# Turned token rows by way of DRAM in five transfers a chunk, ordered behind the residual sums

## The chip, the cores and the metric

The kernel runs on one core of one Trainium2 chip. The time is the device time of one execution in microseconds (us). Before the change it is 790.7 us, the median of 3 runs (790.24 to 791.23). Engines are named as in the profile: PE (matrix multiplication, with PEld for its weight loads), DVE or VectorE, ACT or ScalarE, POOL or GpSimd, and SP, which here only issues DMAs.

## The reference

Four layers are applied to x of 2048 tokens x 576 features: linear attention, MLP, linear attention, MLP, each on the layer norm of x and with a residual sum. Both attention layers have the same weights, and so have both MLPs.

```python
def _A_ref(x, wqkv, wo):            # 32 heads of 18
    q, k, v = split(x @ wqkv)
    phi = lambda t: where(t > 0, t + 1, exp(t)) + 1e-6
    pq, pk = phi(q), phi(k)
    kv = einsum("bhsd,bhse->bhde", pk, v);  z = pk.sum over tokens
    num = einsum("bhqd,bhde->bhqe", pq, kv)
    den = einsum("bhqd,bhd->bhq", pq, z)[..., None] + 1e-6
    return (num / den) @ wo
def _B_ref(x, w1, b1, w2, b2):      # 576 -> 4608 -> 576
    h = gelu(layernorm(x) @ w1 + b1)
    return h @ w2 + b2
x = x + _A_ref(_layernorm(x), A_wqkv, A_wo)
x = x + _B_ref(_layernorm(x), B_w1, B_b1, B_w2, B_b2)
x = x + _A_ref(_layernorm(x), A_wqkv, A_wo)
x = x + _B_ref(_layernorm(x), B_w1, B_b1, B_w2, B_b2)
```

## The kernel before

Layers are called 1 to 4 here; in the code `li` runs from 0 to 3. Layers 1 and 3 are attention (`layer_A`), 2 and 4 the MLP (`LayerB`). Tokens go in 16 tiles of 128, and four tiles make a chunk of 512 columns. All weights stay in SBUF. The residual x lives in a DRAM buffer `x_d` in float32; each tile's sum (L379) is stored there by SP (L385) and loaded again where it is needed (L366 for the residual, L265 for a norm).

Every matmul against tokens needs the normed rows turned, features on partitions: that is `yT`, 128 x 5 x 2048. `LNPipe` makes it. An item is a token tile; each `tick` moves every item one stage on: load (L265, where the row is not at hand), statistics (L272, L273, L278, L281/L283), the reciprocal root on POOL (L288), for POOL norms a small product (L292), the norm into `y_ring` (L303 on POOL, L307 on VectorE, with a copy of the last 64 features by POOL, L311), and the turn. There are two ways to turn:

- by PE: five transposes (L324) into a PSUM bank of their own, `ps_tp`, and a copy by ScalarE (L326). Layer 1 does so for all tiles, and the first chunk of each MLP too (fed at L528 from the output stage of the attention layer before).
- by DMA (`turn_rows`): VectorE transposes blocks of 32 x 32 (L225) into the single buffer `turned`; with the fourth tile of a chunk SP issues 16 SBUF to SBUF copies (L232) in pieces of 256 bytes, which put the blocks on the right partitions. The columns of a chunk then stand in another order, which `spread` and `gather` undo where ScalarE reads the result. Chunks 1 to 3 of each MLP and all four chunks of layer 3 take this way: 10 chunks, 160 copies.

An attention layer first makes k, v and q for all tiles, then the denominators (`den_stage`), the scaling (`scale_stage`) and, tile by tile, the output product and its residual sum (`wo_stage`). While the output stage runs, the sums of tiles 0 to 3 are normed and turned for the following MLP, whose first matmul needs all of chunk 0. Sums are written into `xn`, three buffers.

An MLP layer takes each chunk in turn: nine groups of the first product (`m1_group`, 36 matmuls each, L624) with GELU on ScalarE (L620), then four token tiles of the second product (72 matmuls each, L672) and their residual sums. While chunk c is in its first product, `feed_next` sends the rows of chunk c + 1 into `LNPipe`. Only for c = 0 has it `after=dve_last["sum"]`, an order without a semaphore: the loads and statistics of chunk 1 come after the attention layer's last sum. For later chunks there is no such order.

PSUM has eight banks: two pairs for accumulation (`accA`, `accB`), three single banks `ps_h` and one `ps_tp`.

The order of an engine's instructions is fixed when the kernel is built. PE's order is written out by hand (`pe`). On the other queues, SP's among them, a planner goes through the program with estimated durations and lets instructions that it takes to be ready go ahead of earlier ones that wait; `add_manual_dep(..., NOSYNC)` forbids that for one pair. At run time each queue works strictly in that order.

Of the kernel before, what the change touches and what calls it, by code (L numbers as in the profile page):

```python
# [7 lines left out]
ACT = mybir.ActivationFunctionType  # L8
ALU = mybir.AluOpType
BF16 = mybir.dt.bfloat16  # L10
# [24 lines left out]
def build(tc, A_x, A_wqkv, A_wo, B_w1, B_b1, B_w2, B_b2, out, dbg=None, n_layers=4):  # L35
    nc = tc.nc
    dbg = dbg or {}
    with ExitStack() as ctx:
        const = ctx.enter_context(tc.tile_pool(name="const", bufs=1))
        ps_h = ctx.enter_context(tc.tile_pool(name="ps_h", bufs=3, space=PSUM))  # L40
        ps_tp = ctx.enter_context(tc.tile_pool(name="ps_tp", bufs=1, space=PSUM))
# [21 lines left out]
        eps_row = const.tile([1, H], BF16, name="eps_row")  # L63
        one_row = const.tile([1, P], BF16, name="one_row")
# [9 lines left out]
        def inner_diag(tile_, lead, n):  # L74
# [10 lines left out]
            fill(eps_row, 1e-6),  # L85
# [30 lines left out]
        x_d = dpool.tile([NT, P, D], F32, name="x_d")  # L116

# [99 lines left out]
        state = dict(ycnt=0, vcnt=0, xl=0)  # L217
# [3 lines left out]
        def turn_rows(y, t, kind):  # L221

            c, j = divmod(t, TPC)
            nb = 4 * KD if kind == "B" else D // 32
            nc.vector.transpose(out=turned[:, 0:nb, j, :], in_=y[:, 0:32 * nb])  # L225
            if j < TPC - 1:
                return
            for i in range(4):
                for jj in range(4):
                    nk = KD if 16 + jj < nb else KD - 1  # L230
                    cols = slice(c * CB + i * P, c * CB + (i + 1) * P)
                    nc.sync.dma_start(  # L232
                        out=yT[32 * jj:32 * (jj + 1), 0:nk, cols],
                        in_=turned[32 * i:32 * (i + 1), jj:4 * (nk - 1) + jj + 1:4].rearrange("p k t c -> p k (t c)"))
# [8 lines left out]
        class LNPipe:  # L243
# [11 lines left out]
            def tick(self, transposes=1):  # L255
                for it in list(self.items):
# [58 lines left out]
                    elif st == 4:  # L315
                        y = it["y"]
                        t = it["t"]
                        if it["evac"] == "dma":
                            turn_rows(y, t, it["kind"])
                            self.items.remove(it)  # L320
                            continue
                        tp = ps_tp.tile([P, KD, P], BF16, name="tp", tag="tp")
                        for k in range(KD):
                            pe(nc.tensor.transpose(out=tp[:, k, :], in_=y[:, k * P:(k + 1) * P], identity=ident[:]))  # L324
                        if it["evac"] == "act":
                            nc.scalar.copy(out=yT[:, :, t * P:(t + 1) * P], in_=tp[:])  # L326
                        else:
                            nc.vector.tensor_copy(out=yT[:, :, t * P:(t + 1) * P], in_=tp[:])
                        self.items.remove(it)
                        continue  # L330
# [41 lines left out]
        def residual(li, t, halves):  # L372
            xo = xo_of.pop((li, t))
            last = (li == n_layers - 1)
            if last:
                xn = work.tile([P, 2 * D], BF16, name="xbf", tag="xn", bufs=3)[:, 0:D]
            else:
                xn = work.tile([P, D], F32, name="xn", tag="xn", bufs=3)[:]
            total = nc.vector.tensor_tensor(out=xn.rearrange("p (h n) -> p h n", h=2), in0=halves,  # L379
                                            in1=xo.rearrange("p (h n) -> p h n", h=2), op=ALU.add)  # L380
            dve_last["sum"] = total.ins.name
            if last:
                nc.sync.dma_start(out=out_f[t * P:(t + 1) * P, :], in_=xn)
                return None
            nc.sync.dma_start(out=x_d[t], in_=xn)  # L385
            return xn

        def layer_A(li, next_kind, pre_a1=None):
# [129 lines left out]
            def wo_stage(t):  # L518
# [8 lines left out]
                if xn is not None and next_kind == "B" and t < TPC:  # L527
                    lnp.feed(xn, t, "B", "pool", "act")  # L528
# [46 lines left out]
        class LayerB:  # L575
# [7 lines left out]
            def m1_group(self, c, g):  # L583
# [32 lines left out]
                def evict(n):  # L616
                    f = g * GF + n
                    hT[f] = blk.tile([P, D], BF16, name="hT", tag="blk")
                    to, ps = (hT[f][:, 0:CB], dst[n]) if c == 0 else (spread(hT[f][:, 0:CB]), gather(dst[n]))
                    act_last["gelu"] = nc.scalar.activation(out=to, in_=ps, func=ACT.Gelu_apprx_tanh,  # L620
                                                            bias=b1T[:, f:f + 1], scale=1.0).ins.name
# [24 lines left out]
            def run(self):  # L646
                li, next_kind = self.li, self.next_kind

                def feed_next(c, i):
                    if c + 1 < NCB:  # L650
                        t = (c + 1) * TPC + i
                        lnp.feed(None, t, "B", "dve", "dma", load_from=t, after=(dve_last["sum"] if c == 0 else None))

                for c in range(NCB):
# [12 lines left out]
                    for j in range(TPC):  # L667
                        t = c * TPC + j
                        acc = ps_acc.tile([P, 2, 512], F32, name="m2_ps", tag=next_acc())
                        for f in range(NF):  # L670
                            for half in range(2):
                                pe(nc.tensor.matmul(acc[:, half, 0:HALF], lhsT=hT[f][:, j * P:(j + 1) * P],  # L672
                                                    rhs=w2_sb[:, f, half * HALF:(half + 1) * HALF],
                                                    start=(f == 0), stop=(f == NF - 1)))
# [111 lines left out]
```

## Time and profile before

| | |
|---|---|
| median of 3 runs | 790.7 us |
| the profiled execution | 790.27 us, its span 788.6 us |
| granted PE clock, mean | 0.992 |
| busy: PE / VectorE / ScalarE / POOL | 769.9 / 275.4 / 341.7 / 127.0 us |
| first matmul of the MLP (layers 2, 4) | 112.1 and 491.9 us |
| one MLP chunk | 70.4 us: 35 first product, 35.4 second |
| DMA | 63.2 MB, mean 80 GB/s |

The page of the profile gives busy times by engine and slices of the span in tenths. The waits name who waited for whom, in total, how often and the longest. The timelines give start and duration of merged instructions of one engine, and in brackets the idle time ahead of them and who ended it. For SP a line is the time in which it issued such DMAs one after another; the data land later.

### The profile page before, as it was taken

The page shows a single profiled execution, that of the slowest core. Times are in us where ns is not written, and L with a number is a line of the kernel's source. Part 1 is how long each engine was busy: PE and PEld are TensorE (multiplying, and loading weights), DVE is VectorE, ACT ScalarE, POOL GpSimd, SP SyncE. Part 2 cuts the span into 40 slices and gives each one's busy share as a digit, 9 for nine tenths or more (in the row PEclk, how much of TensorE's full clock was granted, in tenths as well). Part 3 has the DMA queues.
Part 4 walks back from the last instruction along what each step waited for, and adds up shares of the span by engine and source line. Part 5 has one row for each costly group of instructions (what it writes and reads, how often), then busy time and mean ns, then how long its engine had stood idle before and what let it go on. Part 6 is the DMA issues. An engine that isn't in the chain of part 4 may idle for free.

```text
span 788.6 us, 15939 instructions
## 1 busy us (share of the span) xinstructions
PE 769.9 (98%) x6613; PEld 496.5 (63%) x6613; DVE 275.4 (35%) x710; ACT 341.7 (43%) x754; POOL 127.0 (16%) x211
## 2 busy tenths in 40 slices
PE   8999999999999999999999999996999999999998
PEld 5776654675477457547777756455744764675476
DVE  6786864044324413301355597544100000000000
ACT  5888636304610650362077774650056016304600
POOL 4671403013000301200000022311110010001000
PEclk9999999999999999999999999998899999999999
DMA  9990473122412331311120028443410110011000
GB/s 265 280 294 5 130 252 91 22 75 66 94 43 69 83 65 46 91 17 31 61 61 2 1 89 288 152 94 79 86 39 1 31 61 2 5 50 38 1 24 23
DMA packets 70642, 63.23 MB, mean 80 GB/s; under 512 B 37418, under 2 KB 55210, under 8 KB 70570
## 3 DMA queue, kind: packets, MB, share of 16 engines
q1 hardware_dynamic: 70570, 62.21, 28.1%
q8 instruction: 52, 0.85, 0.4%
q14 instruction: 20, 0.16, 0.1%
HBM read 39.38 MB, written 16.52 MB: 71 GB/s over the span
## 4 chain that ended last, share of the span: by engine, by line
PE 83%; DVE 7%; DMA 4%; SPq 3%; POOL 1%; issue 1%; ACT 1%; DVEq 0%; POOLq 0%
PE m_ps L672 34%; PE h_ps L624 17%; PE hp_ps L624 14%; PE q_ps L436 5%; PE k_ps L400 5%; PE v_ps L415 3%; SPq L232 3%; PE v_ps L412 2%; PE wo_ps L523 2%; DVE xn L379 1%; DMA x_d<-xn 1%; DVE turned L225 1%; PE kvacc L430 1%; DMA x_ring<-x_d 1%; DVE y_ring L307 1%
## 5 line engine op out<-in xcount | busy, mean ns | idle before, releaser
L672 PE MATMUL m_ps<-w_sb,hT 128*128 128x288 bf16 x2304 | 286.2, 287 | 8.5 <-DVE xbf L379 8.5
L672 PEld LDWEIGHTS <-hT 128*128 128x128 bf16 x2304 | 225.9, 98 | 69.8 <-issue 12.1
L624 PEld LDWEIGHTS <-w_sb 64*128 64x128 bf16 x2304 | 124.4, 94 | 136.6 <-issue 1.9
L624 PE MATMUL hp_ps<-yT,w_sb 64*128 64x512 bf16 x1152 | 178.0, 376 | 0.0
L629 ACT COPY relay_sb<-relay_sb 128x1 f32<-128x1 f32 x144 | 28.5, 198 | 276.6 <-PE h_ps L624 234.7
L624 PE MATMUL h_ps<-yT,w_sb 64*128 64x512 bf16 x1152 | 147.9, 376 | 0.0
L620 ACT ACTIVATE hT<-h_ps,b1T 128x512 bf16<-128x512 f32 x144 | 91.2, 684 | 44.5 <-PE h_ps L624 44.5
L288 POOL TENSOR_TENSOR ln_rstd<-ln_u,neg_half 128x1 f32<-128x1 f32 x64 | 36.2, 567 | 413.9 <-DVE ln_u L281 216.8
L620 ACT ACTIVATE hT<-hp_ps,b1T 128x512 bf16<-128x512 f32 x144 | 91.2, 693 | 0.0
L379 DVE TENSOR_TENSOR xbf<-m_ps,x_ring 128x576 bf16<-128x576 f32 x16 | 12.0, 754 | 221.2 <-PE m_ps L672 221.2
L369 POOL TENSOR_TENSOR x_ring<-x_ring,b_bc 128x576 f32<-128x576 f32 x32 | 41.1, 1291 | 203.7 <-DMA x_ring<-x_d 203.6
L379 DVE TENSOR_TENSOR xn<-m_ps,x_ring 128x576 f32<-128x576 f32 x16 | 12.1, 758 | 155.9 <-PE m_ps L672 155.9
L624 PE MATMUL h_ps<-yT,w_tail 64*128 64x512 bf16 x144 | 54.1, 376 | 0.0
L624 PE MATMUL hp_ps<-yT,w_tail 64*128 64x512 bf16 x144 | 54.1, 376 | 0.0
L436 PE MATMUL q_ps<-yT,wqkv_sb 128*126 128x512 bf16 (+1 forms) x200 | 50.0, 382 | 0.5 <-ACT phi_a L351 0.5
L225 DVE STREAM_TRANSPOSE turned<-y_ring 128x640 bf16<-128x640 bf16 (+1 forms) x40 | 32.2, 812 | 41.8 <-DMA yT<-turned 35.4
L523 PE MATMUL wo_ps<-kvwo,pq 126*128 126x288 bf16 (+1 forms) x320 | 43.7, 285 | 2.1 <-DVE xn L379 1.6
L400 PE MATMUL k_ps<-wqkv_sb,yT 128*128 128x288 bf16 x320 | 44.3, 286 | 0.0
L350 ACT ACTIVATE phi_e<-k_ps 128x288 bf16<-128x288 f32 x64 | 27.0, 421 | 34.8 <-PE k_ps L400 34.7
L352 DVE TENSOR_SCALAR phi_e<-phi_e 128x288 bf16<-128x288 bf16 (+2 forms) x104 | 30.7, 296 | 25.3 <-ACT phi_e L350 24.9
L523 PEld LDWEIGHTS <-pq 126*128 126x128 bf16 (+1 forms) x320 | 30.5, 97 | 13.7 <-issue 3.9
L400 PEld LDWEIGHTS <-yT 128*128 128x128 bf16 x320 | 30.9, 98 | 11.1
(90 smaller groups left out, 625.7 us busy)
## 6 DMA issues: line engine op xcount, KB each, us to landing
x_ring<-x_d SPq DMA_DIRECT2D x72, 288.0 KB, 3.1
x_d<-xn SPq DMA_DIRECT2D x48, 288.0 KB, 2.2
w_sb<-in_B_w_dram SPq DMA_DIRECT2D x6, 864.0 KB, 9.5
yT<-turned SPq DMA_DIRECT2D x128, 40.0 KB, 2.0
w_sb<-in_B_w_dram SPq DMA_DIRECT2D x9, 512.0 KB, 5.5
x<-in_A_x_dram SPq DMA_DIRECT2D x16, 144.0 KB, 4.1
x_ring<-in_A_x_dram SPq DMA_DIRECT2D x16, 144.0 KB, 3.4
out_dram<-xbf SPq DMA_DIRECT2D x16, 144.0 KB, 1.8
```

The costliest lines, as they stand in the source:

```text
L225: nc.vector.transpose(out=turned[:, 0:nb, j, :], in_=y[:, 0:32 * nb])
L288: nc.gpsimd.tensor_tensor(out=rstd[:], in0=it["u"][:], in1=neg_half[:], op=ALU.pow)
L352: nc.vector.tensor_scalar(out=e[0:rows, 0:n], in0=e[0:rows, 0:n], scalar1=1.0, scalar2=1e-6, op0=ALU.min, op1=ALU.add)
L369: nc.gpsimd.tensor_tensor(out=xo, in0=xo, in1=b2_bc[:], op=ALU.add)
L379: total = nc.vector.tensor_tensor(out=xn.rearrange("p (h n) -> p h n", h=2), in0=halves, in1=xo.rearrange("p (h n) -> p h n", h=2), op=ALU ...
L400: pe(nc.tensor.matmul(kp[:, 0:HALF], lhsT=yT[:, k, tok], rhs=wqkv_sb[:, k, D + half * HALF: D + (half + 1) * HALF], start=(k == 0), stop=( ...
L436: pe(nc.tensor.matmul(qp[0:GR[g], :], lhsT=wqkv_sb[:, k, GO[g]:GO[g] + GR[g]], rhs=yT[:, k, c * CA:(c + 1) * CA], start=(k == 0), stop=(k ...
L523: pe(nc.tensor.matmul(wp[:, half, 0:HALF], lhsT=pq[(g, c)][0:GR[g], j * P:(j + 1) * P], rhs=kvwo[g][0:GR[g], half * HALF:(half + 1) * HALF ...
L620: act_last["gelu"] = nc.scalar.activation(out=to, in_=ps, func=ACT.Gelu_apprx_tanh, bias=b1T[:, f:f + 1], scale=1.0).ins.name
L624: mm = pe(nc.tensor.matmul(dst[n], lhsT=wt, rhs=mv, start=(seen[n] == 0), stop=(seen[n] == 8)))
L629: relay = nc.scalar.copy(out=relay_sb[:, 1:2], in_=relay_sb[:, 0:1])
L672: pe(nc.tensor.matmul(acc[:, half, 0:HALF], lhsT=hT[f][:, j * P:(j + 1) * P], rhs=w2_sb[:, f, half * HALF:(half + 1) * HALF], start=(f == ...
```

## The change

All rows of layers 2 to 4 are turned by DMA; layer 1 keeps PE's transposes. The 16 copies of a chunk become four writes to a DRAM buffer `y_d` (two, in turn), one for each 32 partitions of `turned`, and one read of the whole chunk into `yT`, which waits for the four writes. Every turn stands behind the residual sum that was last written in the program (`dve_last["sum"]`, order only), and `feed_next` has `after=dve_last["sum"]` for every chunk. GELU reads chunk 0 in the turned order as it does the others. `ps_tp` goes; `ps_h` has four banks, and layer 1's transposes take theirs from it. The constants `eps_row` and `one_row` of the denominator's last matmuls get 126 rows instead of one, with zeros in all rows of `eps_row` but the first. The last token tile of layer 4 does its 36 matmuls of the first half of columns and then those of the second, and each half has its own sum and its own store.

```diff
-        ps_h = ctx.enter_context(tc.tile_pool(name="ps_h", bufs=3, space=PSUM))
-        ps_tp = ctx.enter_context(tc.tile_pool(name="ps_tp", bufs=1, space=PSUM))
+        ps_h = ctx.enter_context(tc.tile_pool(name="ps_h", bufs=4, space=PSUM))
...
-        eps_row = const.tile([1, H], BF16, name="eps_row")
-        one_row = const.tile([1, P], BF16, name="one_row")
+        eps_row = const.tile([126, H], BF16, name="eps_row")
+        one_row = const.tile([126, P], BF16, name="one_row")
...
-            fill(eps_row, 1e-6),
+            fill(eps_row, 0.0),
+            lambda: nc.gpsimd.memset(eps_row[0:1, :], 1e-6),
...
+        y_d = [dpool.tile([KD, P, CB], BF16, name=f"y_d{i}") for i in range(2)]
...
-        def turn_rows(y, t, kind):
+        def turn_rows(y, t):
 
             c, j = divmod(t, TPC)
-            nb = 4 * KD if kind == "B" else D // 32
-            nc.vector.transpose(out=turned[:, 0:nb, j, :], in_=y[:, 0:32 * nb])
+            turn = nc.vector.transpose(out=turned[:, :, j, :], in_=y[:])
+            if dve_last["sum"] is not None:
+                tc.add_manual_dep(turn.ins, dve_last["sum"], NOSYNC, reason="rows are turned behind the sums")
             if j < TPC - 1:
                 return
+            home = y_d[state["turns"] % 2]
+            state["turns"] += 1
             for i in range(4):
-                for jj in range(4):
-                    nk = KD if 16 + jj < nb else KD - 1
-                    cols = slice(c * CB + i * P, c * CB + (i + 1) * P)
-                    nc.sync.dma_start(
-                        out=yT[32 * jj:32 * (jj + 1), 0:nk, cols],
-                        in_=turned[32 * i:32 * (i + 1), jj:4 * (nk - 1) + jj + 1:4].rearrange("p k t c -> p k (t c)"))
+                nc.sync.dma_start(
+                    out=home[:, :, i * P:(i + 1) * P].rearrange("k (jj r) n -> r (k jj) n", jj=4),
+                    in_=turned[32 * i:32 * (i + 1), :, :, :].rearrange("r j t c -> r j (t c)"))
+            nc.sync.dma_start(out=yT[:, :, c * CB:(c + 1) * CB], in_=home.rearrange("k p n -> p k n"))
...
-                        tp = ps_tp.tile([P, KD, P], BF16, name="tp", tag="tp")
+                        tp = ps_h.tile([P, 512], F32, name="tp", tag="h")
+                        tp = tp[:, 0:DPAD // 2].bitcast(BF16).rearrange("p (k n) -> p k n", k=KD)
...
-            total = nc.vector.tensor_tensor(out=xn.rearrange("p (h n) -> p h n", h=2), in0=halves,
-                                            in1=xo.rearrange("p (h n) -> p h n", h=2), op=ALU.add)
-            dve_last["sum"] = total.ins.name
+            parts = [slice(h * HALF, (h + 1) * HALF) for h in range(2)] if last and t == NT - 1 else [slice(0, D)]
+            for i, cols in enumerate(parts):
+                ps = halves if len(parts) == 1 else halves[:, i:i + 1, :]
+                nh = ps.shape[1]
+                total = nc.vector.tensor_tensor(out=xn[:, cols].rearrange("p (h n) -> p h n", h=nh), in0=ps,
+                                                in1=xo[:, cols].rearrange("p (h n) -> p h n", h=nh), op=ALU.add)
+                dve_last["sum"] = total.ins.name
+                if last:
+                    nc.sync.dma_start(out=out_f[t * P:(t + 1) * P, cols], in_=xn[:, cols])
...
-                    lnp.feed(xn, t, "B", "pool", "act")
+                    lnp.feed(xn, t, "B", "pool", "dma")
...
-                    to, ps = (hT[f][:, 0:CB], dst[n]) if c == 0 else (spread(hT[f][:, 0:CB]), gather(dst[n]))
-                    act_last["gelu"] = nc.scalar.activation(out=to, in_=ps, func=ACT.Gelu_apprx_tanh,
+                    act_last["gelu"] = nc.scalar.activation(out=spread(hT[f][:, 0:CB]), in_=gather(dst[n]),
+                                                            func=ACT.Gelu_apprx_tanh,
...
-                        lnp.feed(None, t, "B", "dve", "dma", load_from=t, after=(dve_last["sum"] if c == 0 else None))
+                        lnp.feed(None, t, "B", "dve", "dma", load_from=t, after=dve_last["sum"])
...
-                        for f in range(NF):
-                            for half in range(2):
-                                pe(nc.tensor.matmul(acc[:, half, 0:HALF], lhsT=hT[f][:, j * P:(j + 1) * P],
+                        by_half = li == n_layers - 1 and t == NT - 1
+                        steps = [(f, half) for half in range(2) for f in range(NF)] if by_half else \
+                            [(f, half) for f in range(NF) for half in range(2)]
+                        for f, half in steps:
+                            pe(nc.tensor.matmul(acc[:, half, 0:HALF], lhsT=hT[f][:, j * P:(j + 1) * P],
...
```

## The prediction

> **What bounds the kernel now.** I read the page first (spans, busy shares, slices), then the list of waits, the timelines of VectorE, SP and PE around the one weak slice, and short windows at the end of the attention layers.
>
> ```profile
> span 788.6 us, 15939 instructions
> ...
> PE 769.9 (98%) x6613; PEld 496.5 (63%) x6613; DVE 275.4 (35%) x710; ACT 341.7 (43%) x754; POOL 127.0 (16%) x211
> ...
> PE   8999999999999999999999999996999999999998
> ```
>
> PE is busy 98% of the span, so only the 18.7 us in which it is idle, and PE work that is removed, can be won. One slice falls to 6 tenths, near 550 us. The waits name its cause (us in total, times, longest):
>
> ```profile
> DVE turned L225 <- DMA yT<-turned: 35.4, 4, 10.3
> ...
> PE m_ps L672 <- DVE xbf L379: 8.5, 1, 8.5
> ```
>
> 8.5 us of PE's idle time is one wait of a second MLP matmul for a residual sum of the last layer. VectorE's timeline (start, us, line, operation, wait before) says why that sum was late:
>
> ```profile
> 537.14 0.58 DVE L307 TENSOR_SCALAR y_ring<-x_ring,ln_mv,ln_rstd 128x576 bf16<-128x576 f32 x1 [0.67 <-POOL ln_rstd L288]
> 545.42 1.57 DVE L225 STREAM_TRANSPOSE turned<-y_ring 128x640 bf16<-128x640 bf16 x2 [7.70 <-DMA yT<-turned]
> ...
> 552.57 1.38 DVE L379 TENSOR_TENSOR xbf<-m_ps,x_ring 128x576 bf16<-128x576 f32 x2
> ```
>
> The sums of tiles 0 and 1 stand behind turns of chunk 3, which is needed 140 us later. Those turns wait until the single buffer `turned` has been read for chunk 2, and SP issues that chunk's copies one by one:
>
> ```profile
> 532.80 10.98 SPq L232 DMA_DIRECT2D yT<-turned  x16
> 543.88 1.01 SPq L265 DMA_DIRECT2D x_ring<-x_d  x2
> 552.71 11.07 SPq L232 DMA_DIRECT2D yT<-turned  x16
> ```
>
> The MLP itself has nothing to give. The places the change can hurt are the ends of the two attention layers, shown here for layer 3 (the second one; PE's timeline, then windows of layers 1 and 3 with PE, PEld, DVE, ACT and POOL busy, granted clock, DMA share, GB/s):
>
> ```profile
> 479.23 0.53 PE L324 MATMUL tp<-ident,y_ring 128*128 128x128 bf16 x5
> 480.01 1.39 PE L523 MATMUL wo_ps<-kvwo,pq 126*128 126x288 bf16 x10 [0.26 <-DVE xn L379]
> ...
> 485.45 6.53 PE L523 MATMUL wo_ps<-kvwo,pq 126*128 126x288 bf16 x50
> 491.91 1.04 PE L624 MATMUL h_ps<-yT,w_sb 64*128 64x512 bf16 x8
> ```
> ```profile
> 104.00:106.00 2.00, 2.00 (x18) 1.51 (x16) 1.66 (x4) 1.39 (x3) 0.00 (x0) 1.00 0.80 251
> 106.00:108.00 2.00, 1.19 (x10) 0.79 (x9) 0.50 (x1) 0.84 (x2) 0.00 (x0) 1.00 0.95 323
> ...
> 486.00:488.00 2.00, 2.00 (x18) 1.58 (x17) 1.37 (x3) 1.72 (x3) 0.00 (x0) 1.00 1.04 408
> 488.00:490.00 2.00, 2.00 (x18) 1.57 (x17) 0.98 (x2) 0.00 (x0) 0.00 (x0) 1.00 1.04 386
> ```
> ```profile
> 553.00:565.00 12.00, 11.66 (x76) 8.49 (x76) 1.20 (x3) 0.00 (x0) 0.00 (x0) 0.78 0.36 58
> ```
>
> Before the first MLP matmul (491.91; after layer 1 at 112.1) the 16 DMA engines are full with residual stores and loads. The last line is a stretch with almost only one chunk's 16 turn copies: 0.36 of 12 us, so 4.3 us of all engines' time, for 0.65 MB in pieces of 256 bytes.
>
> **The change part by part.**
>
> *Order behind the sums.* Loads and statistics of chunks 2 and 3 must now come after the sums of the chunk before, and turns after the sum last written. Nothing of chunk 3 can stand ahead of tile 0's sum: minus 8.5. What is later: the norm of a chunk now starts in its predecessor's MLP. It takes 15 us (497 to 512 on VectorE) and some 10 for the copies, from 8 us into a stretch of 70.4; 37 us to spare, so nothing. I take -8.5; the other end is 0, if another instruction takes the sum's place.
>
> *Five DMAs instead of sixteen, 10 chunks.* SP's share falls from 11 us a chunk to four writes of about 0.6 (row 0.60 each; but three weight loads of 768 pieces took 3.35, 1.1 each, when the engines were full), a wait until they land, and one read. Landing: 2.0 to 2.2 us in calm, 3.2 for stores and 3.9 for loads in the full stretch 476 to 500. A chunk is ready 2.5 + 2.2 + 0.6 + 3.1 = 8.4 us after its last turn, against 11 + 2.0 = 13. For the MLP's chunks 1 to 3 and for layer 3's rows both are hidden: layer 3's last chunk was turned at 398.7 and its k projection comes at 435. Nothing.
>
> *The first chunk of each MLP, now turned too.* Removed: 4 x 5 PE transposes a layer (four steps of 0.28 us between the start of the transposes and that of the next group) and four ScalarE copies of 0.70. Added: four turns of 0.84 on VectorE, which was busy 24.9 of the 30.3 us of this stage; and two trips over DMA, 4.3 us of engine time for the writes (by the row above) and 0.65 MB at 386 GB/s = 1.7 for the read. In layer 3 the turn of tile 3 stands behind the sum of tile 7, which began at 481.53; with the turn of tile 2 ahead of it too, it ends near 484.1 (481.53 + 0.84 + 0.76 + 0.84, and 0.1 of gaps). Behind the turns on VectorE stand the scale products and the sum of tile 8, for which PE waits 0.26 now. Four writes issued to 486.6; landed with 3.2 at 489.8 to 490; read issued 490.5, landed with 3.9 at 494.5. The wo groups alone would let the MLP begin at 492.5 (0.6 late through VectorE), so the copy decides. Behind the read on SP, which waits for the writes, stand the stores of tiles 8 to 12 and their `xn` buffers (three, so the sum of tile 14 waits for the store of 11): that puts PE's second accumulators near the same 494.5. I take +2.8 for layer 3; ends -1.1 (only the PE work is saved) and +6.6 (below). In layer 1 the residual rows that are loaded are bfloat16 and half as long, so the engines are less full, and 1.1 us of PE waiting is there already: turn of tile 3 to 103.1, writes issued to 105.6, landed 108.5, read landed 112.5 to 113, against 112.1. I take +1.0, ends -1.5 and +5.0.
>
> No row shows a write to DRAM in pieces of 256 bytes; nearest are the same pieces between SBUF rows at 4.3 us a chunk (taken) and, as upper end, twice that: the slowest of the 160 old copies landed in 3.8 us against a median of 2.0. The Trainium skill, "DMA: Bandwidth & Descriptors", section "Specifications", says that below 512 bytes the DMA engine does a read-modify-write, and "Why small descriptors are slow (HBM only)" exempts SBUF to SBUF. By that rule the old copies were cheap and the new ones are not, with about 8.6 us for the writes (an estimate), and the time would be the second rival's. No run here shows it.
>
> *Fourth one-bank buffer.* The waits of q_ps for phi_a (0.5 us) end: -0.4. With the transposes' own bank gone, a token tile of layer 1 uses four banks where it used three and one, so nothing is lost; ends 0 and -1.
>
> *`eps_row` over 126 rows.* The four closing matmuls of a denominator took 0.17 us from start to start (469.73 to 469.90), the twenty before them 0.39; at that pace they take 0.08: 8 x 0.09 = 0.7 at most. I take -0.3; ends 0 and -0.7. One more fill on POOL lies in the first weights' time.
>
> *GELU in turned order for chunk 0:* ScalarE was busy 22.7 us in chunk 0 (112 to 147) and 22.3 in chunk 1 (182 to 217), which reads that way already. Nothing.
>
> *Last tile by halves.* The last sum takes 0.76 us, then 1.8 for its store. Half of it takes about 0.4, and the store is half: -0.5; ends 0 and -0.8.
>
> **Sum.** -8.5 - 0.4 - 0.3 - 0.5 + 2.8 + 1.0 = -5.9. The profiled execution took 790.27 (span 788.6 and 1.7 around it), 0.4 below the median of 790.7. That gives 784.4.
>
> **The rivals.**
>
> *Hidden tails.* The two starts of the MLP cost nothing, because the copies land beside the wo groups. For it: 8 us lie between the last turn and 492. Against: the engines at 1.04. The time is 790.3 - 9.7, less half of the 2.2 us of PE transposes: 779.5.
>
> *The small DRAM writes decide (slower).* Place: the last 10 us of both attention layers. At 8.6 us for the writes they land near 494, the read at 498.5 in layer 3: +6.6; in layer 1 +5.0. Total -9.7 + 11.6 = +1.9: 792.2. For it: the engines are full there already. Against: 2560 pieces took only 4.3 us before. It decides as soon as the two starts together come more than 9.7 us later.
>
> *The stall stays or moves.* Another instruction holds the sum of tile 0. Then 790.3 - 1.2 + 3.8 = 792.9. Against: the dependences name exactly the instructions that stood there.
>
> **How the numbers follow.** Chances: forecast 0.54, hidden tails 0.22, small writes 0.16, stall stays 0.08. A difference under 0.2% (1.6 us) is about what can't be told from none. The forecast's own range is 781.5 to 788; with the hidden case below and most of the slower cases it is 778.5 to 792. Faster: 0.54 + 0.22 = 0.76, slightly lowered for an overlap of the small writes' milder half with no change: faster 0.75, same 0.10 (most of it from the small writes), slower 0.15.
>
> **What would show it.** PE's wait for `xbf` is gone and the sums of the last layer's chunk 0 follow their matmuls by under 1 us; the turns of chunk 2 come after 565. SP shows groups of four writes and one read. In the attention layers the first MLP matmul waits for `yT` 1 to 4 us, with the DMA share at 1.0 before it. If the writes land over 5 us after issue, the second rival is right; if the first MLP matmul follows the last wo group at once, the first. I am wrong if the order of the queues changes elsewhere: a residual load or a store put behind the waiting read would stall every later sum.

## The result and the profile after

The changed kernel takes 799.0 us (median of 4 runs, 797.5 to 799.5) where the kernel before takes 790.9 (4 runs beside it, 790.2 to 791.2). The ratio is 1.010, with a 95% interval of 1.0083 to 1.0118: the change makes the kernel slower by 8.1 us. The forecast was 784.4 us, and 792.0 was the top of its range.

The page of the profile after, with the same rows as before and the row of the granted clock in tenths:

```profile
span 797.7 us, 15688 instructions
...
PE 770.2 (97%) x6573; PEld 495.9 (62%) x6573; DVE 278.3 (35%) x719; ACT 335.7 (42%) x746; POOL 126.6 (16%) x212
...
PE   7999869999999999999999997799999999999998
PEclk9999979999999999999999999699999999999999
```

The weak slice at 550 us is gone. Two others have come, near 110 us and from 480 to 518 us, which are the ends of the two attention layers, and in both the granted clock falls too. PE's busy time is what it was (770.2 against 769.9), though 40 matmuls are gone, because the matmuls under the low clock take longer. Cut at PE's first matmul of each layer (starts in its timeline), the two spans compare like this:

| stretch | before | after | difference |
|---|---|---|---|
| start to the k product of tile 3 (17.4 / 18.4) | 17.4 | 18.4 | +1.0 |
| rest of layer 1, to layer 2's first matmul (112.1 / 121.0) | 94.7 | 102.6 | +7.9 |
| layer 2, to layer 3's first matmul (393.8 / 402.7) | 281.7 | 281.7 | 0 |
| layer 3, to layer 4's first matmul (491.9 / 511.9) | 98.1 | 109.2 | +11.2 |
| layer 4 to the end (788.6 / 797.7) | 296.7 | 285.8 | -10.9 |

So the stall that the change removes was worth 10.9 us, and the ends of the attention layers took 19 back. (The first row is not counted as the change's: these k products wait for the first rows of x to be loaded and normed, and tile 3's begins between 17.1 and 20.0 us in the kernels shown here, whatever their edit.)

The waits on the list of after that matter (us in total, times, longest):

```profile
DVE xn L386 <- DMA x_d<-xn: 18.9, 7, 4.7
PE wo_ps L531 <- DVE xn L386: 16.7, 11, 4.0
```

Before, these two were 4.3 and 1.6 us. No line says that a first MLP matmul waits for `yT`. What is late is not the turned chunk but the stores of the residual rows: a sum of the output stage cannot write its `xn` buffer until the store that last read it has landed, and PE waits for the sum to empty its accumulator. In layer 3, VectorE's timeline (start, us, line, operation, wait before) shows the turn of tile 3, on which the whole chunk waits, and the sums of tiles 11 and 12:

```profile
491.19 0.82 DVE L225 STREAM_TRANSPOSE turned<-y_ring 128x640 bf16<-128x640 bf16 x1
...
500.80 0.76 DVE L386 TENSOR_TENSOR xn<-wo_ps,x_ring 128x576 f32<-128x576 f32 x1 [4.09 <-DMA x_d<-xn]
506.21 0.76 DVE L386 TENSOR_TENSOR xn<-wo_ps,x_ring 128x576 f32<-128x576 f32 x1 [4.65 <-DMA x_d<-xn]
```

SP's timeline for the same time tells why the stores are late:

```profile
492.04 3.52 SPq L233 DMA_DIRECT2D y_d<-turned  x4
495.61 0.95 SPq L369 DMA_DIRECT2D x_ring<-x_d  x1
496.66 0.74 SPq L393 DMA_DIRECT2D x_d<-xn  x1
498.33 0.37 SPq L236 DMA_DIRECT2D yT<-y_d  x1
498.75 0.52 SPq L369 DMA_DIRECT2D x_ring<-x_d  x1
499.32 0.42 SPq L393 DMA_DIRECT2D x_d<-xn  x1
```

The store at 496.66 is that of tile 8, whose sum ended at 492.65: it stood 4.0 us behind the issue of the four writes and of one load. It lands just before 500.80, where the sum of tile 11 takes its buffer. The store at 499.32 is that of tile 9 (sum ended 493.99). It stood behind SP's wait for the writes, behind the read and behind another load. The chain of work that ended last (start and length, us; for a DMA, from issue to landing) goes through this store in layer 3, and in layer 1 through the one that was issued right behind the read:

```profile
104.93 3.72 DMA y_d<-turned
109.29 6.40 DMA x_d<-xn
116.63 4.39 PE wo_ps L531 x20
...
494.86 3.40 DMA y_d<-turned
499.32 6.70 DMA x_d<-xn
507.02 4.96 PE wo_ps L531 x20
```

Tile 9's store takes 6.7 us to land, and the sum of tile 12 begins at 506.21. PE's timeline shows both waits:

```profile
496.44 1.39 PE L531 MATMUL wo_ps<-kvwo,pq 126*128 126x288 bf16 x10 [0.61 <-DVE xn L386]
501.61 2.56 PE L531 MATMUL wo_ps<-kvwo,pq 126*128 126x288 bf16 x10 [3.79 <-DVE xn L386]
507.02 4.96 PE L531 MATMUL wo_ps<-kvwo,pq 126*128 126x288 bf16 x20 [2.85 <-DVE xn L386]
511.91 1.47 PE L632 MATMUL h_ps<-yT,w_sb 64*128 64x512 bf16 x8
```

The first MLP matmul follows the last output product at once. After the wait of 3.79 us the same ten matmuls take 2.56 us instead of 1.39. Windows of 2 us (columns: length, PE, PEld, DVE, ACT, POOL busy, granted clock, DMA share, GB/s) give the reason:

```profile
496.00:498.00 2.00, 1.39 (x10) 0.97 (x10) 0.71 (x2) 0.72 (x2) 0.00 (x0) 1.00 1.15 182
498.00:500.00 2.00, 0.00 (x0) 0.00 (x0) 0.00 (x0) 0.00 (x0) 0.00 (x0) 0.79 0.83 286
500.00:502.00 2.00, 0.39 (x2) 0.25 (x2) 0.76 (x1) 0.00 (x0) 0.00 (x0) 0.50 0.79 136
502.00:504.00 2.00, 2.00 (x10) 1.18 (x8) 0.00 (x0) 0.00 (x0) 0.00 (x0) 0.50 1.00 320
```

In layer 3 the clock falls while PE waits, and it is back only when the MLP has begun. PE's last output product before the wait ends at 497.83; in windows of 0.5 us the clock is 1.00 until 499.0, 0.67 in the next window and 0.50 from there to 512.5. So it fell 1.3 us after PE had stopped. In layer 1 it fell 1.8 us after, and in the stall of layer 4 before, 3.2 us after. The Trainium skill, "TensorE: Matmul & The Clock Gate", Part 1, says that PE falls to half rate after an idle window of about 3.4 us. The traces agree that waits of 3.79 us here and 8.5 before halve the clock; they don't agree on the length, since it fell 1.3 us into the first of them.

Added up for the end of layer 3, from the output products of tiles 3 and 4 to the first MLP matmul (478.23 to 511.91 here, 469.90 to 491.91 before, so 11.7 us more): PE's waits are 0.42 + 0.38 + 1.04 + 0.81 + 0.61 + 3.79 + 2.85 = 9.9, where PE was idle 0.8 us before: +9.1. The last 30 matmuls at the low clock take 2.56 + 4.96 instead of 30 x 0.131 (the row of 50 in 6.53 before): +3.6. Off go 1.1 us of transposes. That is +11.6. The table's 11.2 for the whole layer is half a us less, which the layer had won by 478.23.

Layer 4's gain is larger than the wait of 8.5 us for the same reason: before, the clock fell after that wait too. Windows of before:

```profile
553.00:556.00 3.00, 2.66 (x12) 1.68 (x12) 0.95 (x2) 0.00 (x0) 0.00 (x0) 0.50 0.28 45
556.00:560.00 4.00, 4.00 (x25) 2.81 (x24) 0.00 (x0) 0.00 (x0) 0.00 (x0) 0.72 0.42 66
```

PE's 2.66 us at half the clock and 4 us at 0.72 cost 2.66 x 0.5 + 4 x 0.28 = 2.5 us; 8.5 + 2.5 = 11.0, against 10.9 in the table.

### The profile page after: what moved, and what is told of

Its sections match the earlier page's. It is cut to its first block, busy times and chain, and to the rows that moved or that the text cites. A ratio compares the mean times of both kernels' runs of the same rounds, so it can differ in the third digit from the quotient of the medians.

```text
span 797.7 us, 15688 instructions
## 1 busy us (share of the span) xinstructions
PE 770.2 (97%) x6573; PEld 495.9 (62%) x6573; DVE 278.3 (35%) x719; ACT 335.7 (42%) x746; POOL 126.6 (16%) x212
## 4 chain that ended last, share of the span: by engine, by line
PE 88%; DVE 4%; DMA 3%; ACT 1%; POOL 1%; issue 1%; SPq 1%; DVEq 0%; POOLq 0%; ACTq 0%
PE m_ps L682 35%; PE h_ps L632 20%; PE hp_ps L632 16%; PE k_ps L408 5%; PE q_ps L444 4%; PE v_ps L423 3%; PE v_ps L420 2%; DMA x_d<-xn 2%; PE wo_ps L531 2%; DVE xn L386 1%; PE kvacc L438 1%; DMA y_d<-turned 1%; PE tp L327 1%; SPq L233 1%; POOL y_ring L305 1%
## 5 line engine op out<-in xcount | busy, mean ns | idle before, releaser
L386 DVE TENSOR_TENSOR xbf<-m_ps,x_ring 128x576 bf16<-128x576 f32 (+1 forms) x17 | 12.2, 722 | 217.7 <-PE m_ps L682 217.7
L386 DVE TENSOR_TENSOR xn<-m_ps,x_ring 128x576 f32<-128x576 f32 x16 | 12.1, 758 | 176.9 <-PE m_ps L682 176.9
L531 PE MATMUL wo_ps<-kvwo,pq 126*128 126x288 bf16 (+1 forms) x320 | 50.6, 312 | 17.8 <-DVE xn L386 16.7
L531 PEld LDWEIGHTS <-pq 126*128 126x128 bf16 (+1 forms) x320 | 33.4, 105 | 35.1 <-issue 21.0
L225 DVE STREAM_TRANSPOSE turned<-y_ring 128x640 bf16<-128x640 bf16 x48 | 39.9, 834 | 13.6 <-POOL y_ring L313 12.9
```

The costliest lines, as they stand in the source:

```text
L225: turn = nc.vector.transpose(out=turned[:, :, j, :], in_=y[:])
L386: total = nc.vector.tensor_tensor(out=xn[:, cols].rearrange("p (h n) -> p h n", h=nh), in0=ps, in1=xo[:, cols].rearrange("p (h n) -> p h n ...
L531: pe(nc.tensor.matmul(wp[:, half, 0:HALF], lhsT=pq[(g, c)][0:GR[g], j * P:(j + 1) * P], rhs=kvwo[g][0:GR[g], half * HALF:(half + 1) * HALF ...
```

## The experiments

The account to be tested: the first chunk's writes and its read delay the residual stores on the same queue, the sums wait for the stores, PE for the sums, and the clock falls. Its rivals: the 16 DMA engines are simply too full, whichever queue the stores are on; the turns on VectorE or the order behind the sums cost the time; the small DRAM writes as such do; the turned chunk itself is late.

### The parts that could help, each by itself

First, the change with the first chunk turned by PE again:

```diff
-                    lnp.feed(xn, t, "B", "pool", "dma")
+                    lnp.feed(xn, t, "B", "pool", "act")
...
-                    act_last["gelu"] = nc.scalar.activation(out=spread(hT[f][:, 0:CB]), in_=gather(dst[n]),
-                                                            func=ACT.Gelu_apprx_tanh,
+                    to, ps = (hT[f][:, 0:CB], dst[n]) if c == 0 else (spread(hT[f][:, 0:CB]), gather(dst[n]))
+                    act_last["gelu"] = nc.scalar.activation(out=to, in_=ps, func=ACT.Gelu_apprx_tanh,
```

> The changed kernel, but the first chunk of each MLP is turned by PE and copied by ScalarE as before (and GELU reads it in plain order); all else of the change stays. Store theory (the first chunk's five DMAs in the output stage make the residual stores land late, three xn buffers then hold the sums, PE waits 3.8 and 2.9 us, and its clock falls to half): both output stages return to their length of before, the gain in layer 4 (10.7 us) stays: 779, within 2. The rival that the longer output stages come from something else in the change (four single banks shared with the transposes, the 126-row constants): 790 to 799, with waits of wo_ps for xn of over 5 us in each attention layer.

Measured: 779.65 us, ratio to before 0.9856 (0.9837 to 0.9875). This one part of the change costs 19.4 us, and the rest of it gains 11. The two waits on its list:

```profile
DVE xn L386 <- DMA x_d<-xn: 6.2, 6, 2.1
...
PE wo_ps L531 <- DVE xn L386: 3.1, 4, 1.5
```

Next, the kernel before with nothing but the order of loads and statistics in `feed_next`:

```diff
-                        lnp.feed(None, t, "B", "dve", "dma", load_from=t, after=(dve_last["sum"] if c == 0 else None))
+                        lnp.feed(None, t, "B", "dve", "dma", load_from=t, after=dve_last["sum"])
```

> The kernel before, with one edit: loads and statistics of every later chunk stand behind the last sum. If the order was the cure of layer 4's stall: the 8.5 us and the slow clock after it go, 779.5 within 1.5. If the five DMAs a chunk were the cure (a shorter hold of the buffer of turned blocks): 788 to 791.

Measured: 779.72 us, 0.986 (0.9844 to 0.9875). One line brings all of the gain. Its list has no wait of a second product for a sum any more, and its mean granted clock is 1.000.

The kernel before with five DMAs instead of sixteen, and no order:

```diff
-                for jj in range(4):
-                    nk = KD if 16 + jj < nb else KD - 1
-                    cols = slice(c * CB + i * P, c * CB + (i + 1) * P)
-                    nc.sync.dma_start(
-                        out=yT[32 * jj:32 * (jj + 1), 0:nk, cols],
-                        in_=turned[32 * i:32 * (i + 1), jj:4 * (nk - 1) + jj + 1:4].rearrange("p k t c -> p k (t c)"))
+                nc.sync.dma_start(
+                    out=home[:, :, i * P:(i + 1) * P].rearrange("k (jj r) n -> r (k jj) n", jj=4),
+                    in_=turned[32 * i:32 * (i + 1), :, :, :].rearrange("r j t c -> r j (t c)"))
+            nc.sync.dma_start(out=yT[:, :, c * CB:(c + 1) * CB], in_=home.rearrange("k p n -> p k n"))
```

> The kernel before, with the sixteen copies of a chunk replaced by four writes to DRAM and one read, for the same ten chunks, and no new order. If the hold of the buffer of turned blocks was the cause of the stall, two holds get shorter by some 6 us each and the sum of tile 0 is in time: 780 within 2. If only the order cures it: 788 to 791, with a wait of m_ps for xbf of over 6 us left.

Measured: 780.18 us, 0.9861 (0.9841 to 0.9882). It cures the stall as well. The turns of a later chunk still stand ahead of the sums, but they wait only for four writes, 2.8 us at most. VectorE's timeline has these two turns of layer 4 that wait for writes; the sum that was late before comes at 541.25, and PE's second products run on without a wait:

```profile
520.62 1.57 DVE L225 STREAM_TRANSPOSE turned<-y_ring 128x640 bf16<-128x640 bf16 x2 [1.02 <-DMA y_d<-turned]
...
533.59 1.57 DVE L225 STREAM_TRANSPOSE turned<-y_ring 128x640 bf16<-128x640 bf16 x2 [0.74 <-DMA y_d<-turned]
```

Order or fewer DMAs, either is enough, and the two together gain no more than one.

Last, the first experiment with the 16 copies of before, so that neither the DMAs nor the first chunk are changed, but the order, the fourth one-bank buffer, the 126 rows of `eps_row` and the halves are there:

```diff
-                nc.sync.dma_start(
-                    out=home[:, :, i * P:(i + 1) * P].rearrange("k (jj r) n -> r (k jj) n", jj=4),
-                    in_=turned[32 * i:32 * (i + 1), :, :, :].rearrange("r j t c -> r j (t c)"))
-            nc.sync.dma_start(out=yT[:, :, c * CB:(c + 1) * CB], in_=home.rearrange("k p n -> p k n"))
+                for jj in range(4):
+                    nc.sync.dma_start(
+                        out=yT[32 * jj:32 * (jj + 1), :, c * CB + i * P:c * CB + (i + 1) * P],
+                        in_=turned[32 * i:32 * (i + 1), jj:4 * (KD - 1) + jj + 1:4].rearrange("p k t c -> p k (t c)"))
```

> All of the change but its two DMA parts: sixteen copies as before and the first chunk by PE, with the new order, four single banks, the 126-row constants and the last tile by halves. Against the order alone (779.7) the three small parts should bring 0.4 + 0.3 + 0.5 by my prediction's own terms: 778.5. If they bring nothing: 779.7.

Measured: 779.53 us, 0.9853 (0.9838 to 0.9867). Against the order alone (779.72) the three small parts bring nothing that can be measured: the four runs lie from 779.0 to 779.8, those of the order alone from 779.0 to 780.2. For the halves, VectorE's timeline of after shows why: the two half sums run together after the last matmul, as one did before, and from there to the end of the span it is 3.4 us instead of 3.6.

```profile
794.34 0.82 DVE L386 TENSOR_TENSOR xbf<-m_ps,x_ring 128x288 bf16<-128x288 f32 x2 [8.06 <-PE m_ps L682]
```

### What in the first chunk's new way costs the time

VectorE's share: the first experiment again, with the eight turns of the two first chunks made on VectorE beside PE's, and read by nobody.

```diff
+                        if it["norm"] == "pool" and it["kind"] == "B":
+                            extra = nc.vector.transpose(out=turned[:, :, t % TPC, :], in_=y[:])
+                            tc.add_manual_dep(extra.ins, dve_last["sum"], NOSYNC, reason="rows are turned behind the sums")
```

> The kernel of the first experiment (first chunk by PE) with four more turns a layer on VectorE, behind the sums as in the change, into the buffer of turned blocks, which nobody reads there. VectorE's part of the loss by itself: with four turns of 0.84 us in each output stage and waits of wo_ps for xn and rden_ps for quad_rden of 2.65 us a layer seen in the changed kernel, I expect 2 to 5 us more than the first experiment, 782 to 785. If the turns are free, under 780.5; if they carry the loss, over 790.

Measured: 780.83 us in one run, 1.2 above the median without them (its four runs go up to 780.3) and less than the 2 to 5 I expected. The turns and their order are not it.

The read's share: the change without the first chunk's read.

```diff
+            if read:
-            nc.sync.dma_start(out=yT[:, :, c * CB:(c + 1) * CB], in_=home.rearrange("k p n -> p k n"))
+                nc.sync.dma_start(out=yT[:, :, c * CB:(c + 1) * CB], in_=home.rearrange("k p n -> p k n"))
...
-                            turn_rows(y, t)
+                            turn_rows(y, t, read=it["norm"] != "pool")
```

> The changed kernel without the read of the first chunk (left out: yT keeps its old columns there, so the MLPs work on wrong rows for 512 tokens; everything else is as changed). Queue theory: the stores stand behind 4.1 us of writes only, not behind 2.9 us of the read too; the second wait of each output stage (1.8 and 2.9 us) goes, the first (4.0 and 3.8) stays, and with it most of the slow clock: 791 to 795. If the writes alone carry the loss: 797 or more.

Measured: 791.77 us (10 runs), 1.0017 of before (1.0007 to 1.0028). Step by step that is PE's way 779.65, with turns 780.8, with turns and writes (and without PE's transposes) 791.8; the read on top makes 799.0. Of the two long waits of PE in layer 3, the second is gone (its PE timeline):

```profile
498.61 5.43 PE L532 MATMUL wo_ps<-kvwo,pq 126*128 126x288 bf16 x30 [4.29 <-DVE xn L387]
```

So the first wait is made by the four writes, and the second by the read together with SP's wait ahead of it, although nothing on PE waits for what it reads. Stores are not all that comes late behind the writes: in layer 1 of this run VectorE's longest wait, 5.0 us for the sum of tile 11, is put down to the load of its residual row.

One `xn` buffer more (and one buffer less at two other places, for room):

```diff
...
-                xn = work.tile([P, D], F32, name="xn", tag="xn", bufs=3)[:]
+                xn = work.tile([P, D], F32, name="xn", tag="xn", bufs=4)[:]
...
```

> The changed kernel with four xn buffers instead of three; room is made by two instead of three buffers for phi_e and for the rows of v, which may cost some us in the first stage of the attention layers (read the output stages alone). Store theory: each sum of the output stage may run one store further ahead, so the waits of xn for x_d stores (18.9 us in total) and of wo_ps for xn (16.7) fall by at least half. VectorE theory (the four turns of 0.84 us are what delays the sums): both change by less than a fifth.

Measured: 797.33 us in one run, with 16.7 us of waits for stores and 14.1 us of PE's for sums (18.9 and 16.7 without it). I had expected at least half of them to go. The direction fits the account, the size doesn't: a fourth buffer gives a store the time of one more tile, 1.3 us here (the sums of tiles 8 and 9 lie that far apart), and the stores are late by more than that (tile 8's is issued 4.0 us late, tile 9's 5.3, and that one then takes 6.7 to land). By itself this run tells little.

The 16 SBUF copies in place of the five DMAs, with the first chunk still by DMA (`turn_rows` as in the diff of the fourth experiment above):

> The changed kernel with the old sixteen SBUF to SBUF copies for every chunk in place of four writes and one read; order, first chunk by DMA and all else as changed. Form theory (pieces of 256 bytes into DRAM, and the second trip, are the price): the output stages recover at least 6 of the 19 us, 793 or less. Queue theory (any large block of transfers ahead of the residual stores in SP's queue delays them; sixteen issues take 11 us of SP): no better, 797 to 806.

Measured: 803.7 us in one run, 4.7 more than the change. SP's and PE's timelines in layer 3:

```profile
495.12 10.29 SPq L232 DMA_DIRECT2D yT<-turned  x16
```
```profile
510.50 5.94 PE L529 MATMUL wo_ps<-kvwo,pq 126*128 126x288 bf16 x30 [10.38 <-DVE xn L384]
```

Here there is no DRAM in the first chunk's way and no read that waits for writes, and the loss is larger: the stores stand 10.3 us behind the issues. While they stand there, from 498 to 506 us, the 16 engines are busy only 0.28 to 0.50 of each us. So a loss like this needs neither writes to DRAM nor engines that are full while the stores stand; a queue that is held is enough.

### Taking the stores or the chunk to another queue

The first chunk's five DMAs issued by ScalarE:

```diff
-                nc.sync.dma_start(
+                eng.dma_start(
...
-            nc.sync.dma_start(out=yT[:, :, c * CB:(c + 1) * CB], in_=home.rearrange("k p n -> p k n"))
+            eng.dma_start(out=yT[:, :, c * CB:(c + 1) * CB], in_=home.rearrange("k p n -> p k n"))
...
-                            turn_rows(y, t)
+                            turn_rows(y, t, nc.scalar if it["norm"] == "pool" else None)
```

> The changed kernel, but the first chunk's four writes and read are issued by ScalarE instead of SP; the residual stores and loads stay on SP. Queue theory (stores stand in one line behind 4.1 us of writes and 2.9 us of the read): stores overtake, waits of wo_ps for xn fall from 16.7 us to under 8, the time to 784 to 792. Capacity theory (the 16 engines simply have 7 us more to move in a full stretch, whoever issues): the stores land as late, 795 or more.

Measured: 793.76 us in one run, above the 784 to 792 that I expected. The sums' waits for stores do fall from 18.9 to 3.2 us, and PE's for sums from 16.7 to 3.9. But the issuing engine now has the block in its own way. ScalarE's timeline in layer 3:

```profile
490.62 7.08 ACTq L234 DMA_DIRECT2D y_d<-turned  x4
497.74 1.55 ACT L523 CAST rden_bc<-rden_ps 126x512 bf16<-126x512 f32 x3 [7.01 <-DMA x_ring<-x_d]
```

The casts of the inverse denominators stand behind the four issues for 7.0 us. The scale products wait for those, and PE for them, 3.8 us at once (in layer 1 a first MLP matmul also waits 2.8 us for `yT`). As PE is held there, the later sums come later too and leave the stores more time, so part of the fall may be due to that:

```profile
PE wo_ps L532 <- DVE pq L524: 6.0, 3, 3.8
...
PE wo_ps L532 <- DVE xn L387: 3.9, 7, 1.0
```

The same with GpSimd as the issuer (`nc.gpsimd` in the last line of the diff):

> The same with GpSimd issuing the first chunk's four writes and read. Queue theory: waits of wo_ps for xn under 8 us, 784 to 793, unless GpSimd needs so long for the issue that the first matmul of the MLP waits for yT instead. Capacity theory: 795 or more.

Measured: 826.92 us in one run, far from the 784 to 793 expected. Now the chunk itself is late, which it was in none of the others to that extent:

```profile
PE h_ps L633 <- DMA yT<-y_d: 29.6, 2, 15.4
```

GpSimd's timeline and the chain of layer 3 show that the issue is not what takes the time:

```profile
506.12 2.80 POOL L234 DMA_DIRECT2D y_d<-turned  x4 [4.40 <-DVE turned L226]
527.15 1.27 POOL L373 TENSOR_TENSOR x_ring<-x_ring,b_bc 128x576 f32<-128x576 f32 x1 [18.23 <-DMA x_ring<-x_d]
```
```profile
531.33 5.49 DMA yT<-y_d
```

GpSimd issues the four writes in 2.8 us, but the read only 22 us later: ahead of it in its queue stand bias sums of the MLP (L373), and the first of them waits 18.2 us for a residual row that SP loads behind the stores. (In layer 1 it is 16.4 us.) So what the 29.6 us of PE's waits for `yT` show is this order, not a slow issue by GpSimd. And the stores stay late, though the block is no longer in their queue: VectorE still waits 12.1 us for them and PE 13.5 us for sums, where under 8 was expected. That speaks for the full engines.

And the other way round, the chunk on SP and the attention layers' stores on ScalarE's queue:

```diff
-            nc.sync.dma_start(out=x_d[t], in_=xn)
+            (nc.scalar if li % 2 == 0 else nc.sync).dma_start(out=x_d[t], in_=xn)
```

> The changed kernel, but the residual stores of the attention layers are issued by ScalarE, so that they no longer stand behind the first chunk's writes in SP's queue; the five DMAs and the residual loads stay on SP. Queue theory: the stores land in under 4 us, waits of xn for x_d stores fall from 18.9 us to under 6; what is left is the wait for the loads of tiles 12 to 15 behind the chunk, or for yT: 782 to 792. Capacity theory: stores as late as before, 796 or more.

Measured: 793.94 us in one run, 5.1 less than the change and between the two ranges that I had given. The waits for stores fall to 9.8 us (under 6 was expected), those of PE for sums to 7.9. From 480 to 508 us the stores on ScalarE's queue land in 5.1 us by the median, those of the change in 4.0 (484 to 512) and those before in 3.2 (476 to 500). New are sums that wait for residual rows, whose loads still stand on SP behind the block (3.5 and 4.2 us), and a first MLP matmul that waits 2.7 us for `yT`. In each of these versions whatever stands behind the block pays: with ScalarE's queue as the second one, 5 us are won either way, and neither gets back to the 779.7 of PE's way. With the waits that remain here and in GpSimd's version, the held queue is not the whole cause: the full engines have a share that these runs do not measure.

### The clock

The change with eleven more matmuls of 128x512, whose result nobody reads, ahead of the output products of tiles 13 and 14 in both attention layers:

```diff
+                if t in (13, 14):
+                    fill_ps = ps_h.tile([P, 512], F32, name="fill_ps", tag="h")
+                    for _ in range(11):
+                        pe(nc.tensor.matmul(fill_ps[:], lhsT=head_bc[:, 0, :], rhs=quad_mask[:].rearrange("p j n -> p (j n)"),
+                                            start=True, stop=True))
```

> The changed kernel with eleven idle matmuls of 512 columns (2.4 us at full clock, results unread) before the output products of tiles 13 and 14 in each attention layer, that is inside PE's long waits. If the fall of the granted clock to 0.50 after those waits is a cost of its own, the stores still set when the sums run, the added matmuls cost nothing, and the clock stays at 1.00: 791 to 796, although PE has more to do. If the slow clock only fills time that the stores would take anyway: 798 to 802.

Measured: 795.64 us (4 runs), 1.0057 of before (1.0042 to 1.0072): 3.4 us less than the change, with 44 matmuls more. Windows of layer 3:

```profile
500.00:502.00 2.00, 1.95 (x10) 0.92 (x10) 0.00 (x0) 0.00 (x0) 0.00 (x0) 1.00 0.99 324
502.00:504.00 2.00, 0.33 (x2) 0.05 (x1) 0.52 (x1) 0.00 (x0) 0.00 (x0) 1.00 1.05 407
```

Where the change had a clock of 0.50, it is 1.00 until 504 (0.61 and 0.54 in the 4 us after, when PE has waited 1.96 us once more). So of the 19 us lost at least 3.4 are the clock, a consequence of the waits and not part of them.

## Why the prediction was wrong

*The stall of layer 4.* That it would go was right. Its term, -8.5, was too small, since it left out the clock that fell after it: -10.9. And I had put it down to the order, with the five DMAs at nothing; the runs show that either alone does it.

*Later chunks and layer 3's rows.* That they are hidden was right: layer 2 takes 281.7 us in both, and the kernels with the order alone, with five DMAs alone and with both agree within 0.7 us.

*The first chunk.* This is the step that failed: +2.8 for layer 3 and +1.0 for layer 1, where 11.2 and 7.9 were measured. The working followed the chunk itself, and that part came out well. With the 8.8 us by which layer 3 now starts later, the turn of tile 3 was to end at 492.9 and did at 492.0; the read was to be issued at 499.3 and was at 498.3. But the sentence "so the copy decides" was wrong, and with it the sign I gave, a wait of 1 to 4 us for `yT`: there is none. What decides is in the half sentence on the stores of tiles 8 to 12 and their three `xn` buffers. I saw that they stand behind the read, and let them end "near the same 494.5" without adding them up. Tile 9's store, from the rows above: issued 1.0 us after the read (499.3), landed 6.7 later instead of the 3.2 assumed. That gives a sum of tile 12 at 506.2, and the output products of two tiles still to come on a PE at half clock. The forecast's own moment for layer 4's first matmul, moved by 8.8, was 503.5; it came at 511.9.

What each part of the miss in layer 3 was worth can be estimated from the forecast's own times and the rows. A store 1.0 us behind the read at 490.5, with the assumed 3.2, lands at 494.7; the sum ends at 495.5, and two tiles of 1.31 us later it is 498.1, which is +6.2 and not +2.8. So the forecast was too small already for not adding up. The store was then issued 1.0 us earlier than that, took 3.7 us longer until its sum began, and the last 20 matmuls took 4.96 us instead of 2.62 at the low clock: 6.2 - 1.0 + 3.7 + 2.3 = 11.2, as in the table.

*The clock.* It was in no term, on neither side of the sum: the forecast had a row of 0.78 in front of it and did not ask where it came from.

*VectorE.* 0.6 late was taken in layer 3; the turns by themselves cost some 1.2 in the two layers, in a single run.

*The small parts.* -0.4, -0.3 and -0.5 were taken; together they measured nothing (779.53 against 779.72). The half sums were not earlier at all: their own row says they waited for the last matmul together.

*The rivals.* The sign that was to show "hidden tails", a first MLP matmul right behind the last output product, came true while both starts came later, so it could not tell the two cases apart. "The small DRAM writes decide" had the right place and the right sign, at +11.6 for the two stages instead of 19.1, and the wrong mechanism. Its own sign, writes that land over 5 us after issue, did not come: they took 3.4 us by the median and 4.1 at most. It needed 8.6 us of engine time for a chunk's writes. In a calm chunk of layer 4 after (windows of 3 us; the DMA share is the last column but one) SP issues the four writes from 600.60 and the read at 606.03, and nothing else is on its way:

```profile
600.00:603.00 3.00, 3.00 (x32) 1.36 (x28) 0.57 (x1) 1.83 (x4) 0.00 (x0) 1.00 0.51 78
603.00:606.00 3.00, 3.00 (x32) 1.36 (x28) 0.00 (x0) 1.81 (x6) 0.00 (x0) 1.00 0.86 146
```

That is 0.51 x 3 + 0.86 x 3 = 4.1 us for the writes, no more than the 4.3 of the old copies. It was right to take the row. The Trainium skill, "DMA: Bandwidth & Descriptors", section "Specifications", says that below 512 bytes the DMA engine does a read-modify-write; these writes show no price for it over the copies between SBUF rows, 4.1 us against 4.3. The last sentence of the forecast's signs, that a store put behind the waiting read would stall every later sum, is what happened, though the first of the two long waits came from the writes alone; it should have been a rival with a price.

Open remains how the delay of tile 9's store divides between the full engines (their share of busy time is 0.79 to 1.02 there in windows of 2 us) and the order in which a queue is served. The sixteen copies show a loss from a held queue with engines half idle, and GpSimd's version shows late stores with nothing of the block in their queue; no run separates the two in the change itself.

## What to carry to other kernels

When a block of DMAs is put on a queue, add up the time of what stands behind it (issue, the wait inside the block, landing) and follow each of those to the engine that waits for its buffer; that, and not when the block itself is ready, was worth 19 us here. When PE is to wait some 3 us or more, or a wait of that length is removed, the slow clock after it belongs in the sum (2.5 us behind layer 4's stall, at least 3.4 at the ends of the two attention layers). And try the smallest part alone: one order without a semaphore, 779.7 us, beats both the kernel before (790.9) and the whole change (799.0).

## What the runs showed of the hardware

- Writes to DRAM in pieces of 256 bytes took 4.1 us of the engines' time for 0.65 MB, no more than the same pieces between SBUF rows (4.3).
- A store of 288 KB that lands in 2.2 us by the median takes 6.7 when it is issued behind such a block and its read.
- Every wait of PE of 3.2 us or more brought its granted clock to 0.50, between 1.3 and 4.8 us after PE had stopped (windows of 0.5 us). Of the shorter ones one of 2.0 us did so (the filler's layer 3), and those of 1.8 (its layer 1) and 1.5 (PE's way) did not. In the change the clock stayed low for 13.5 us in layer 3 and 10.2 in layer 1, as matmuls and waits alternated.
- In layer 3 the same four writes took 3.5 us to issue on SP, 5.5 on SP when ScalarE issued the stores beside it, 7.1 on ScalarE beside SP, and 2.8 on GpSimd. Issued by GpSimd they landed in 6.0 us by the median, on SP in 3.6.
